# Layer 2's first product by Strassen's scheme in the last two passes, with split weights stored and fetched

## The chip, the core and the metric

The kernel runs on one core of a Trainium2 chip. A core has a matrix engine (PE; its weight loads are shown apart as PEld), three engines for elementwise work (DVE, ACT, POOL), and a queue for transfers (SP). Each runs its own instructions in the order in which the program lists them, and waits for the others by semaphores. The metric is the device time of one execution in microseconds (us).

## What is computed

Attention with a hash mask, then two feed-forward layers on 1536 tokens of width 512:

```python
x = attention(q, k, v, proj)                       # 1536 x 512
g = x @ w_gate; x = (g * sigmoid(g) * (x @ w_val)) @ w_out        # layer 1, d_ff 1536
h = x @ w_in                                       # layer 2, first product, 512 x 2048
g = max(h, 0) + alpha * min(h, 0)
out = g @ w_out2                                   # layer 2, second product, 2048 x 512
```

All inputs are float32.

## The kernel before

The tokens are cut into three chunks of W = 512. Attention runs interleaved with stage 1 (layer 1) of the first two chunks; then come stage 1 of chunk 2 and three passes of `stage2` (layer 2), for the chunks 1, 2 and 0. Chunk 0 is kept in device memory meanwhile (`spill`) and read back after the first pass. Only the last 270 us, stage 1 of chunk 2 and the three passes, are touched by most of the change.

Every product works on split numbers: a high part h (ACT copies to the matmul type, `split_h`, `w_h`) and a low part l, the rest (DVE or POOL subtracts, `split_l`, `w_l`). A product is three matmuls, h h, h l and l h (`mm3`, L699 to L701; `mm_out`, L704 to L706).

In `stage2`, F2 = 16 blocks f of 128 rows of h are made one after another. A block is 4 k-blocks x 3 matmuls of 512 columns into one PSUM bank (tags G, Y, G, po in turn). DVE forms the leaky g (`leak`, `leak_sum`), ACT and POOL split it (`gh`, `gl`), and D2 = 3 blocks later 12 matmuls add it to four output banks (tags S, S, S, T). At the end of a pass ACT and DVE copy these to `ob`, and SP stores them.

The weights come as a sequence `seq` of tiles (128 x 512) that `w_next` takes one by one. `w_ahead` runs in front of it by the numbers of `LEAD`: load, convert, high part, low part. For layer 2 the converted weights stay in SBUF (`fin.w`); each pass splits all 32 tiles anew, into `wb2` tiles with WB[2] = 6 buffers. Twelve of the 32 were converted early and are read from `whole` (L587); the rest are fetched raw and converted during stage 1 and the first pass (`w_late`, L596 to L601).

A scheduler sets the order of each engine's instructions from the program and the dependencies; a few are pinned. A tile's buffer is taken over once all readers of its last holder are done.

## Time and profile before

| | us |
|---|---|
| median of 3 runs (844.59 to 848.46) | 845.87 |
| the profiled execution | 843.88 |
| its span | 842.0 |

The page of the profile gives for each engine its busy time; further views give the same for a stretch, single instructions in order of time, waits, and the cost of groups of instructions by line. A matmul's busy time contains the wait for its pipeline, so matmuls overlap in the records; the distance between two starts is what one costs. The passes of layer 2 lie at 575.4 to 663.7, 663.7 to 750.7 and 750.7 to 837.7 us of the span.

### The profile page before, as it was taken

What the parts mean: (1) busy time and instruction counts of PE and PEld (TensorE: products, weight loads), DVE (VectorE), ACT (ScalarE), POOL (GpSimd) and SP (SyncE); (2) the same over time, 40 slices, a digit from 0 to 9 for tenths busy, and PEclk for the clock granted to TensorE, in tenths of its full rate; (3) what the DMA queues carried; (4) which work ended last, traced back from release to release, by engine and by line L of the source; (5) the groups of instructions that cost most, each with busy time, mean ns of one, the idle gap of its engine ahead of it and who ended that gap; (6) DMA issues with size and microseconds to landing.
All of it is one profiled execution on the core that took longest, in us unless ns stands there. A gap on an engine that the chain in (4) does not pass through costs nothing.

```text
span 842.0 us, 11156 instructions
## 1 busy us (share of the span) xinstructions
PE 813.0 (97%) x3988; PEld 681.7 (81%) x3988; DVE 536.6 (64%) x826; ACT 442.7 (53%) x738; POOL 347.5 (41%) x284
## 2 busy tenths in 40 slices
PE   5998899998999999999999999999999999999998
PEld 4777778887888888888888888887888888888886
DVE  5889998887898866656675342348986533334332
ACT  7889877877766645555544232224433333333331
POOL 5133337666755633222221352333543354445441
PEclk9999999999999999999999999999999999999999
DMA  9223346867656547554554787784300300010001
GB/s 246 69 69 98 128 120 203 253 220 241 219 202 234 174 152 260 199 179 149 175 188 141 249 286 235 262 282 170 138 1 0 151 1 0 1 51 1 0 1 51
DMA packets 57287, 122.03 MB, mean 145 GB/s; under 512 B 16912, under 2 KB 29200, under 8 KB 56720
## 3 DMA queue, kind: packets, MB, share of 16 engines
q1 hardware_dynamic: 56080, 118.51, 42.3%
q0 software_dynamic: 1008, 2.75, 1.6%
q8 instruction: 32, 0.52, 0.3%
q14 instruction: 23, 0.19, 0.1%
q10 hardware_dynamic: 144, 0.05, 0.0%
HBM read 94.03 MB, written 27.26 MB: 144 GB/s over the span
## 4 chain that ended last, share of the span: by engine, by line
PE 70%; DVE 9%; DMA 7%; ACT 7%; issue 4%; POOL 1%; SPq 0%; DVEq 0%; ACTq 0%; POOLq 0%
PE po L358 9%; PE gp L699 8%; PE gp L701 8%; PE gp L700 8%; PE op L705 5%; PE op L706 5%; PE op L704 5%; DMA raw<-in_wblk_dram 5%; PE hp L700 5%; PE hp L699 5%; PE hp L701 5%; PE S L304 2%; PE S L305 2%; ACT se L306 2%; DVE wt L599 1%
## 5 line engine op out<-in xcount | busy, mean ns | idle before, releaser
L694 POOL TENSOR_TENSOR gl<-ex,gh 128x512 fp32r<-128x512 f32 x81 | 110.2, 1360 | 191.8 <-ACT gh L691 174.5
L358 PE MATMUL po<-se,vv 128*128 128x256 f32 x576 | 139.2, 381 | 5.4 <-ACT se L347 2.8
L691 ACT ACTIVATE gh<-ex 128x512 fp32r<-128x512 f32 x84 | 53.0, 631 | 137.1 <-DVE ex L688 86.6
L358 PEld LDWEIGHTS po<-se,vv 128*128 128x128 f32 x576 | 106.2, 190 | 22.7 <-ACT se L347 4.6
L699 PE MATMUL gp<-xh,wb 128*128 128x512 f32 x288 | 120.1, 417 | 0.5 <-ACT xh L383 0.5
L701 PE MATMUL gp<-xh,wb 128*128 128x512 f32 x288 | 112.9, 392 | 0.0
L700 PE MATMUL gp<-xl,wb 128*128 128x512 f32 x288 | 112.7, 391 | 0.0
L636 ACT ACTIVATE wb<-w 128x512 fp32r<-128x512 f32 x96 | 59.7, 628 | 71.4 <-PE hp L701 57.6
L601 POOL TENSOR_TENSOR wt<-wt,wr 128x512 int32<-128x512 int32 x48 | 63.4, 1327 | 81.1 <-DVE wt L599 32.8
L685 DVE TENSOR_SCALAR ex<-hp,al 128x512 f32<-128x512 f32 x48 | 35.9, 748 | 93.2 <-PE hp L701 92.0
L306 ACT ACTIVATE se<-S 128x512 f32<-128x512 f32 x144 | 81.9, 593 | 23.7 <-PE S L305 22.7
L304 PE MATMUL S<-QA,kt 128*128 128x256 f32 x288 | 79.6, 303 | 6.8 <-ACT se L306 3.0
L341 DVE SCALAR_TENSOR_TENSOR se<-se,mb 128x1536 f32<-128x1536 f32 x48 | 83.5, 1740 | 3.4 <-PE mb L336 3.4
L347 ACT ACTIVATE se<-se 128x1536 f32<-128x1536 f32 x48 | 71.1, 1482 | 8.8 <-DVE se L341 8.6
L705 PE MATMUL op<-wb,gh 128*128 128x512 f32 x192 | 74.8, 390 | 0.9 <-DVE wb L643 0.9
L305 PE MATMUL S<-qb,kt 76*128 76x256 f32 x288 | 73.9, 286 | 1.0 <-ACT kt L218 0.6
L706 PE MATMUL op<-wb,gl 128*128 128x512 f32 x192 | 74.7, 389 | 0.0
L699 PE MATMUL hp<-xh,wb 128*128 128x512 f32 x192 | 74.7, 389 | 0.0
L700 PE MATMUL hp<-xl,wb 128*128 128x512 f32 x192 | 74.7, 389 | 0.0
L701 PE MATMUL hp<-xh,wb 128*128 128x512 f32 x192 | 74.7, 389 | 0.0
L704 PE MATMUL op<-wb,gh 128*128 128x512 f32 x192 | 74.7, 389 | 0.0
L643 DVE TENSOR_TENSOR wb<-w,wb 128x512 fp32r<-128x512 f32 x65 | 56.1, 866 | 17.4 <-ACT wb L636 17.4
(99 smaller groups left out, 1666.7 us busy)
## 6 DMA issues: line engine op xcount, KB each, us to landing
wb<-w SPq DMA_DIRECT2D x72, 512.0 KB, 4.1
raw<-in_wblk_dram SPq DMA_DIRECT2D x68, 512.0 KB, 4.6
w<-wb SPq DMA_DIRECT2D x36, 512.0 KB, 3.0
qr<-in_q_dram SPq DMA_DIRECT2D x24, 256.0 KB, 2.9
nat<-in_k_dram SPq DMA_DIRECT2D x8, 384.0 KB, 3.4
vv<-in_v_dram SPq DMA_DIRECT2D x16, 192.0 KB, 5.6
whole<-wt SPq DMA_DIRECT2D x12, 256.0 KB, 2.2
w<-whole SPq DMA_DIRECT2D x12, 256.0 KB, 4.3
```

The source lines that it names most:

```text
L304: nc.tensor.matmul(pt[:, i, :], lhsT=ka[:, sl], rhs=qa, start=True, stop=False)
L305: nc.tensor.matmul(pt[:, i, :], lhsT=kb[:, sl], rhs=qb, start=False, stop=True)
L306: nc.scalar.activation(out=u.se[:, 2 * j:2 * j + 2, :], in_=pt, func=AF.Copy)
L341: ins = nc.vector.scalar_tensor_tensor(out=u.se, in0=u.se, scalar=FLOOR, in1=u.mx[:, None, :].to_broadcast([P, NC, GQ]), op0=ALU.max, op1= ...
L358: nc.tensor.matmul(it.po[:, u.x, :], lhsT=VV[it.b, it.p][:, kb, u.x * D:u.x * D + P], rhs=u.se[:, kb, :], start=kb == 0, stop=kb == NC - 1)
L694: eng.tensor_tensor(out=l, in0=ex, in1=f32(h), op=ALU.subtract)
L699: nc.tensor.matmul(pt, lhsT=h, rhs=ah, start=first, stop=False)
L700: nc.tensor.matmul(pt, lhsT=h, rhs=al_, start=False, stop=False)
L701: nc.tensor.matmul(pt, lhsT=l, rhs=ah, start=False, stop=last)
L704: nc.tensor.matmul(pt, lhsT=gh, rhs=h, start=first, stop=False)
L705: nc.tensor.matmul(pt, lhsT=gh, rhs=l, start=False, stop=False)
L706: nc.tensor.matmul(pt, lhsT=gl, rhs=h, start=False, stop=last)
```

## The change

The first pass stays as it is, but stores each split tile in device memory (`split`). The second and third pass (`wino`, for the chunks 2 and 0) take two blocks f as a 2 x 2 matrix of weights (two blocks f by two halves of k) and the chunk as a 2 x 2 matrix (two halves of k by two halves of 256 tokens), and form the result from seven products instead of eight, in Winograd's form. Each product is 2 k-blocks x 3 matmuls, now of 256 columns: 42 matmuls a pair of blocks where there were 24 of 512.

The scheme needs sums of weights: two further tiles a pair, made by `w_sums` on DVE from `fin.w`, split by `w_h` and `w_l`, during the second pass, and stored; the third pass fetches them. All other tiles of both passes are fetched (`w_load`). It needs four sums of x (`sums`, split too): those of chunk 2 are made in the first pass from `acc`, those of chunk 0 at the end of the second pass, from an `acc` that is spilled and read back. It needs additions after the products: per pair five on DVE (two of 512 columns, three of 256) after one copy by ACT. The leaky function becomes two Relus on ACT and one step on DVE. POOL splits the low part of g in the middle of the second pass, DVE elsewhere; low parts of layer 2's weights are all DVE's.

The core of the diff:

```diff
...
-LEAD = ((2, 2, 3, 5), (4, 5, 5, 7))
+LEAD = ((2, 2, 3, 5), (4, 5, 5, 7), (4, 4, 5, 6))
...
+    def order2w():
+        o = []
+        for j in range(F2 // 2):
+            o += [F2I + 2 * j, F2S + 2 * j]
+            o += [F2I + F2 + 2 * j - 3] if j > 1 else []
+            o += [F2S + 2 * j + 1]
+            o += [F2I + F2 + 2 * j - 2] if j else []
+            o += [F2I + 2 * j + 1]
+        return o + list(range(F2I + 2 * F2 - 3, F2I + 2 * F2))
+    F2S = F2I + 2 * F2
     o2 = order2()
+    o2w = order2w()
     early = o2[:sum(EARLY)]
     late = [w for w in o2 if w not in early]
-    seq = order1() * NP2 + o2 * NP2
+    seq = order1() * NP2 + o2 + o2w * (NP2 - 1)
     NWT = len(seq)
-    NW1 = NWT - len(o2) * NP2
-    fresh = [w not in seq[:i] for i, w in enumerate(seq)]
-    new = [n or w >= F2I for n, w in zip(fresh, seq)]
+    NW1 = len(order1()) * NP2
+    NW2 = NW1 + len(o2)
+    new = [w not in seq[:i] for i, w in enumerate(seq)]
+    fresh = [n and w < F2S for n, w in zip(new, seq)]
+    split = [dram.tile([P, 2, 512], F32, name=f"s{i}") for i in range(3 * F2)]
     raw, wt, ready = {}, {}, {}
     ws = Bag()
...
             pass
         elif fresh[i] and w in early:
             pin(nc.sync.dma_start(out=fin.w[:, w - F2I, :], in_=whole[w - F2I]))
         elif fresh[i]:
             raw[i] = raw_load(w)
-        elif w < F2I:
-            nc.sync.dma_start(out=f32(w_tile(i)), in_=scratch[w])
+        elif not new[i]:
+            nc.sync.dma_start(out=f32(w_tile(i)), in_=scratch[w] if w < F2I else split[w - F2I])
     def round64(t, a):
...
+        return fin.w[:, w - F2I, n * HW:(n + 1) * HW]
+    def w_sums(i):
+        j, kind = divmod(seq[i] - F2S, 2)
+        f = F2I + 2 * j
+        t = wt[i] = wp.tile([P, 512], F32, tag="wt", name="wt", bufs=WB[0])
+        ops = ((t[:, 0:HW], quarter(f + 1, 0), quarter(f + 1, 1), ALU.add),
+               (t[:, HW:], t[:, 0:HW], quarter(f, 0), ALU.subtract)) if kind == 0 else (
+               (t[:, 0:HW], quarter(f, 0), quarter(f + 1, 0), ALU.subtract),
+               (t[:, HW:], quarter(f, 1), ws.s2, ALU.subtract))
+        if kind == 0:
+            ws.s2 = t[:, HW:]
+        for o, x, y, op in ops:
+            nc.vector.tensor_tensor(out=o, in0=x, in1=y, op=op)
     def w_conv(i):
         w = seq[i]
-        if w >= F2I:
+        if not new[i]:
+            pass
+        elif w >= F2S:
+            w_sums(i)
+        elif w >= F2I:
             wt[i] = fin.w[:, w - F2I, :]
         elif fresh[i]:
             wt[i] = wp.tile([P, 512], F32, tag="wt", name="wt", bufs=WB[0])
...
             n, m = PL
-            eng = nc.gpsimd if i % n < m and not ws.late else nc.vector
+            eng = nc.gpsimd if i < NW1 and i % n < m else nc.vector
             eng.tensor_tensor(out=ready[i][:, 1, :], in0=wt.pop(i), in1=f32(ready[i])[:, 0, :], op=ALU.subtract)
     def w_put(i):
-        if fresh[i] and seq[i] < F2I:
-            nc.sync.dma_start(out=scratch[seq[i]], in_=f32(ready[i]))
+        if new[i]:
+            w = seq[i]
+            nc.sync.dma_start(out=scratch[w] if w < F2I else split[w - F2I], in_=f32(ready[i]))
     def upto(name, n, fn):
         n = min(n, NWT)
...
     def w_ahead(n):
-        lead = LEAD[n >= NW1]
+        lead = LEAD[(n >= NW1) + (n >= NW2)]
         for name, k, fn in (("load", 2, w_load), ("conv", 1, w_conv), ("h", 0, w_h)):
             upto(name, n + lead[0] + k, fn)
         upto("l", n + lead[0], w_l)
...
-    def stage2(c, conv):
+    def sums(acc, ts):
+        def x(k, t):
+            return acc[:, 2 * k:2 * k + 2, t * HW:(t + 1) * HW]
+        f = {}
+        for name, a, b in (("1", lambda: x(0, 1), lambda: x(0, 0)), ("2", lambda: x(1, 1), lambda: f["1"]),
+                           ("4", lambda: x(1, 0), lambda: f["2"]), ("3", lambda: x(1, 1), lambda: x(0, 1))):
+            t = f[name] = wp.tile([P, 2, HW], F32, tag="wr", name="tf", bufs=2)
+            tc.keep_in_program_order(nc.vector.tensor_tensor(out=t, in0=a(), in1=b(), op=ALU.subtract))
+            hl = wp.tile([P, 2, 512], F32R, tag="wb", name="ts", bufs=WB[1])
+            h, l = ts[name] = [hl[:, i, :].rearrange("p (k e) -> p k e", e=HW) for i in range(2)]
+            tc.keep_in_program_order(nc.scalar.activation(out=h, in_=t, func=AF.Copy))
+            (nc.gpsimd if name == "4" else nc.vector).tensor_tensor(out=l, in0=t, in1=f32(h), op=ALU.subtract)
+            yield
+    def out_block(fo, gs, ops):
...
+        a, b_ = gs.pop(fo)
+        if fo == 0:
+            ops.extend(at.ps.tile([P, 512], F32, tag=t, name="op", bufs=at.nb[t]) for t in "SSST")
+        for i in range(W // P):
+            sl = slice(i * P, (i + 1) * P)
+            mm_out(ops[i], a[:, sl], b_[:, sl], h, l, fo == 0, fo == F2 - 1)
+    def out_all(c, ops):
+        for i in range(W // P):
+            out_rows(c * W + i * P, ops[i], i, fin.pool.tile([P, W], F32, tag="ob", name="ob", bufs=4))
...
+    def wino(c, ts, side):
         xh, xl = chunk(c)
-        t0 = c * W
+        def x(k, t):
+            return [v[:, 2 * k:2 * k + 2, t * HW:(t + 1) * HW] for v in (xh, xl)]
+        def product(pt, i, w, n, b):
+            for k in range(2):
+                kk = 2 * n + k
+                mm3(pt[:, i, :], (w[0][:, kk, :], w[1][:, kk, :]), b[0][:, k, :], b[1][:, k, :], k == 0, k == 1)
+        def bank(tag):
+            return at.ps.tile([P, 2, HW], F32, tag=tag, name="hp2", bufs=at.nb[tag])
+        def leaky(f, v):
+            ex = tmp()
+            g = gs[f] = g_tiles()
+            nc.scalar.activation(out=ex, in_=v, func=AF.Relu)
+            nc.scalar.activation(out=v, in_=v, func=AF.Relu, scale=-1.0)
+            nc.vector.scalar_tensor_tensor(out=ex, in0=v, scalar=aln[:, f:f + 1], in1=ex, op0=ALU.mult, op1=ALU.add)
+            split_h(g[0], ex)
+            split_l(g[0], g[1], ex, nc.gpsimd if side and 2 <= f < F2 - 2 else nc.vector)
+        add = ALU.add
+        ops, gs = [], {}
+        for j in range(F2 // 2):
+            pq = fin.pool.tile([P, 2, HW], F32, tag="ob", name="pq", bufs=4)
+            r = wp.tile([P, 4, HW], F32, tag="raw64", name="rs", bufs=RAWB)
+            wa, wb = w_next(), w_next()
+            pt = bank("G")
+            product(pt, 0, wa, 0, x(0, 0))
+            product(pt, 1, wb, 0, ts["1"])
+            nc.scalar.activation(out=pq, in_=pt, func=AF.Copy)
+            pt = bank("Y")
+            product(pt, 0, wb, 1, ts["2"])
+            product(pt, 1, wa, 1, x(1, 0))
+            nc.vector.tensor_tensor(out=r[:, 0:2, :], in0=pt, in1=pq[:, 0:1, :].to_broadcast([P, 2, HW]), op=add)
+            nc.vector.tensor_tensor(out=r[:, 3, :], in0=r[:, 0, :], in1=pq[:, 1, :], op=add)
+            if j == F2 // 2 - 1:
+                for _ in "12":
+                    next(side or iter(()), 0)
+            if j > 1:
+                out_block(2 * j - 3, gs, ops)
+            wb = w_next()
+            pt = bank("G")
+            product(pt, 0, wb, 0, ts["3"])
+            product(pt, 1, wb, 1, x(1, 1))
+            nc.vector.tensor_tensor(out=r[:, 0:3:2, :], in0=pt, in1=r[:, 0::3, :], op=add)
+            x2 = tmp()
+            nc.vector.tensor_tensor(out=x2[:, HW:], in0=r[:, 0, :], in1=pq[:, 1, :], op=add)
+            leaky(2 * j, r[:, 1:3, :].rearrange("p a b -> p (a b)"))
+            if j:
+                out_block(2 * j - 2, gs, ops)
+            wb = w_next()
+            pt = bank("po")
+            product(pt, 0, wb, 1, ts["4"])
+            nc.vector.tensor_tensor(out=x2[:, 0:HW], in0=pt[:, 0, :], in1=r[:, 0, :], op=add)
+            leaky(2 * j + 1, x2)
+        for _ in side or ():
+            pass
+        for f in range(F2 - 3, F2):
+            out_block(f, gs, ops)
+        out_all(c, ops)
...
+                out_block(f - D2, gs, ops)
+            if f % 3 == 2:
+                next(side, 0)
+        out_all(c, ops)
...
-    spill = dram.tile([2, P, KD * W], F32, name="spill")
+    spill = dram.tile([3, P, KD * W], F32, name="spill")
...
-            for i, t in enumerate(chunk(0)):
-                nc.sync.dma_start(out=spill[i], in_=f32(t).rearrange("p k w -> p (k w)"))
+            for i, t in enumerate([f32(t) for t in chunk(0)] + [at.acc]):
+                nc.sync.dma_start(out=spill[i], in_=t.rearrange("p k w -> p (k w)"))
...
         pass
-    for n, c in enumerate((1, 2, 0)):
-        if n == 1:
-            CH.pop(0)
-            for i, t in enumerate(chunk(0)):
-                nc.sync.dma_start(out=f32(t).rearrange("p k w -> p (k w)"), in_=spill[i])
-        ws.late = n == 0
-        stage2(c, late_steps)
+    ts = [{}, {}]
+    aln = fin.pool.tile([P, F2], F32, name="aln")
+    nc.scalar.activation(out=aln, in_=al, func=AF.Copy, scale=-1.0)
+    ws.late = True
+    stage2(1, late_steps, sums(at.acc, ts[0]))
+    ws.late = False
+    CH.pop(0)
+    for i, t in enumerate(chunk(0)):
+        nc.sync.dma_start(out=f32(t).rearrange("p k w -> p (k w)"), in_=spill[i])
+    acc = at.lt.tile([P, KD, W], F32, tag="acc", name="acc", bufs=1)
+    nc.sync.dma_start(out=acc.rearrange("p k w -> p (k w)"), in_=spill[2])
+    wino(2, ts[0], sums(acc, ts[1]))
+    wino(0, ts[1], None)
 # ---- launch: one core; inputs and outputs as the reference has them ----
...
```

What it does to the order of instructions, at three places. In the order `hp_...` is a PSUM bank of the first product, `op` an output bank, `wb_...` a weight tile with its number, `wt` and `w` unsplit weights, `ts` a split sum of x, `rs` and `pq` the additions' tiles, `ex` the leaky tile. Lines of after are those of the changed file.

PE, at the start of the second pass. Before, the pass's first bank ends and the second begins, each with 12 matmuls of 512 columns:

```order
L701 MATMUL hp_6164<-xh,wb_6089 128x512
L699 MATMUL hp_6164<-xh,wb_6089 128x512
L700 MATMUL hp_6164<-xl,wb_6089 128x512
L701 MATMUL hp_6164<-xh,wb_6089 128x512
L699 MATMUL hp_6187<-xh,wb_6104 128x512
L700 MATMUL hp_6187<-xl,wb_6104 128x512
```

After, the second pair's third bank (`hp_6405`, 12 matmuls on the sums tile `wb_6346`), one matmul of its seventh product, and then the pass's first output block:

```order
L739 MATMUL hp_6405<-xl,wb_6346 128x256
L740 MATMUL hp_6405<-xh,wb_6346 128x256
L738 MATMUL hp_6405<-xh,wb_6346 128x256
L739 MATMUL hp_6405<-xl,wb_6346 128x256
L740 MATMUL hp_6405<-xh,wb_6346 128x256
L738 MATMUL hp_6453<-ts,wb_6344 128x256
L743 MATMUL op<-wb_6311,gh 128x512
L744 MATMUL op<-wb_6311,gh 128x512
L743 MATMUL op<-wb_6311,gh 128x512
L744 MATMUL op<-wb_6311,gh 128x512
L743 MATMUL op<-wb_6311,gh 128x512
L745 MATMUL op<-wb_6311,gl 128x512 x2
```

A bank of the first product is now made of two products of six matmuls, and the first output block follows the second pair's third bank.

ACT and DVE at that place. Before, on DVE, behind the copies of the first pass's outputs:

```order
L713 COPY ob<-op 128x512 x2
L643 TENSOR_TENSOR wb_6189<-w_4721,wb_6189 128x512
L685 TENSOR_SCALAR ex_6180<-hp_6164,al 128x512
L688 SCALAR_TENSOR_TENSOR ex_6180<-hp_6164,ex_6180 128x512
L685 TENSOR_SCALAR ex_6203<-hp_6187,al 128x512
```

After, on DVE, from the end of the first pair:

```order
L893 TENSOR_TENSOR ex_6334<-rs,pq 128x256
L900 TENSOR_TENSOR ex_6334<-hp_6349,rs 128x256
L880 TENSOR_TENSOR rs<-hp_6384,pq 128x512
L681 TENSOR_TENSOR wb_6346<-wt,wb_6346 128x512
L863 SCALAR_TENSOR_TENSOR ex_6336<-rs,aln,ex_6336 128x512
L863 SCALAR_TENSOR_TENSOR ex_6357<-ex_6334,aln,ex_6357 128x512
L881 TENSOR_TENSOR rs<-rs,pq 128x256
L733 TENSOR_TENSOR gl<-ex_6336,gh 128x512
```

After, on ACT, from the copy of the first pair's first bank:

```order
L876 ACTIVATE pq<-hp_6282 128x512
L674 ACTIVATE wb_6316<-wt 128x512
L876 ACTIVATE pq<-hp_6370 128x512
L861 ACTIVATE ex_6336<-rs 128x512
L674 ACTIVATE wb_6346<-wt 128x512
L862 ACTIVATE rs<-rs 128x512
L861 ACTIVATE ex_6357<-ex_6334 128x512
L862 ACTIVATE ex_6334<-ex_6334 128x512
L730 ACTIVATE gh<-ex_6336 128x512
```

The split of `wb_6346` stands behind work on the second pair's banks `hp_6370` (its first, on ACT) and `hp_6384` (its second, on DVE).

DVE between stage 1 and the first pass. Before:

```order
L740 TENSOR_TENSOR xl<-acc,xh 128x512
L643 TENSOR_TENSOR wb_5475<-w_4721,wb_5475 128x512
L736 TENSOR_TENSOR acc<-gp,acc 128x512
L740 TENSOR_TENSOR xl<-acc,xh 128x512
L736 TENSOR_TENSOR acc<-gp,acc 128x512
L740 TENSOR_TENSOR xl<-acc,xh 128x512
```

After:

```order
L681 TENSOR_TENSOR wb_5526<-w_4770,wb_5526 128x512
L775 TENSOR_TENSOR acc<-gp,acc 128x512
L635 TENSOR_TENSOR wt<-wt,w_4770 128x256
L635 TENSOR_TENSOR wt<-w_4770 128x256
L635 TENSOR_TENSOR wt<-w_4770,wt 128x256
L779 TENSOR_TENSOR xl<-acc,xh 128x512
L775 TENSOR_TENSOR acc<-gp,acc 128x512
L635 TENSOR_TENSOR wt<-w_4770 128x256
L635 TENSOR_TENSOR wt<-wt,w_4770 128x256
L779 TENSOR_TENSOR xl<-acc,xh 128x512
```

Five sums of weights now stand between the steps that make the x of the first pass.

## Rows read from the trace of the kernel before

**Rows 1.** Page, part 1: busy us, share of the span, instructions.

```profile
PE 813.0 (97%) x3988; PEld 681.7 (81%) x3988; DVE 536.6 (64%) x826; ACT 442.7 (53%) x738; POOL 347.5 (41%) x284
```

**Rows 2.** Busy us, the three passes: PE, PEld, DVE, ACT, POOL; clock, DMA share, GB/s.

```profile
575.40:663.70 88.30, 87.35 (x386) 72.04 (x385) 70.05 (x86) 35.43 (x61) 35.63 (x26) 1.00 0.25 91
663.70:750.70 87.00, 87.00 (x385) 72.06 (x384) 33.36 (x50) 31.37 (x51) 40.64 (x32) 1.00 0.04 13
750.70:837.70 87.00, 87.00 (x385) 71.91 (x383) 32.01 (x48) 28.25 (x46) 36.88 (x29) 1.00 0.03 12
```

**Rows 3.** Waits of PE from 540 us on: total us, times, longest.

```profile
PE op L705 <- DVE wb L643: 0.9, 1, 0.9
```

**Rows 4.** PE in order of time, second pass: start us, us, instruction.

```profile
690.86 0.39 PE L704 MATMUL op<-wb,gh 128*128 128x512 f32 x1
691.09 0.39 PE L705 MATMUL op<-wb,gh 128*128 128x512 f32 x1
```

**Rows 5.** PE in order of time, attention beside stage 1.

```profile
420.59 0.39 PE L701 MATMUL gp<-xh,wb 128*128 128x512 f32 x1
420.82 0.28 PE L304 MATMUL S<-QA,kt 128*128 128x256 f32 x1
...
421.66 0.28 PE L305 MATMUL S<-qb,kt 76*128 76x256 f32 x1
421.78 0.40 PE L699 MATMUL gp<-gh,wb 128*128 128x512 f32 x1
422.02 0.40 PE L700 MATMUL gp<-gl,wb 128*128 128x512 f32 x1
```

**Rows 6.** PE's weight loads in order of time, same stretch.

```profile
420.94 0.19 PEld L304 LDWEIGHTS S<-QA,kt 128*128 128x128 f32 x1
```

**Rows 7.** Groups by line, last two passes: busy us, mean ns, idle before.

```profile
L694 POOL TENSOR_TENSOR gl<-ex,gh 128x512 fp32r<-128x512 f32 x32 | 41.3, 1290 | 78.0 <-ACT gh L691 78.0
L636 ACT ACTIVATE wb<-w 128x512 fp32r<-128x512 f32 x59 | 37.3, 632 | 60.4 <-PE hp L701 53.8 <-PE op L706 4.5
L688 DVE SCALAR_TENSOR_TENSOR ex<-hp,ex 128x512 f32<-128x512 f32 x32 | 21.9, 684 | 0.2
L643 DVE TENSOR_TENSOR wb<-w,wb 128x512 fp32r<-128x512 f32 x30 | 21.1, 704 | 4.2 <-ACT wb L636 4.1
```

**Rows 8.** Groups by line and shape, whole span: 256 columns on DVE, PSUM copies on ACT.

```profile
L380 DVE TENSOR_TENSOR xf<-po,den 64x256 f32<-64x256 f32 x48 | 20.1, 419 | 1.4
L328 DVE TENSOR_TENSOR m<-m 128x256 f32<-128x256 f32 x30 | 15.6, 519 | 0.0
...
L715 ACT ACTIVATE ob<-op 128x512 f32<-128x512 f32 x6 | 3.6, 598 | 8.9 <-PE op L706 8.9
```

**Rows 9.** POOL and DVE in order of time, first pass.

```profile
613.29 1.42 POOL L694 TENSOR_TENSOR gl<-ex,gh 128x512 fp32r<-128x512 f32 x1 [3.21 <-issue]
...
613.71 1.55 DVE L643 TENSOR_TENSOR wb<-w,wb 128x512 fp32r<-128x512 f32 x1 [0.16 <-ACT wb L636]
```

**Rows 10.** DMA issues (KB, median us to landing), and GB/s in 40 slices of 300:330.

```profile
wb<-w SPq DMA_DIRECT2D x72, 512.0 KB, 4.1
...
spill<-xl SPq DMA_DIRECT2D x1, 1024.0 KB, 8.1
...
GB/s 77 0 0 0 0 0 0 0 71 404 224 142 371 186 91 258 0 82 262 382 377 426 360 437 404 350 229 213 289 415 415 366 426 137 27 16 0 109 322 284
```

**Rows 11.** PE and DVE in order of time, stage 1 to first pass; idle before in brackets.

```profile
575.16 0.39 PE L701 MATMUL gp<-gh,wb 128*128 128x512 f32 x1
...
577.65 0.39 PE L700 MATMUL hp<-xl,wb 128*128 128x512 f32 x1
...
574.90 0.69 DVE L740 TENSOR_TENSOR xl<-acc,xh 128x512 fp32r<-128x512 f32 x1 [0.70 <-ACT xh L738]
575.58 0.69 DVE L736 TENSOR_TENSOR acc<-gp,acc 128x512 f32<-128x512 f32 x1
576.97 0.69 DVE L740 TENSOR_TENSOR xl<-acc,xh 128x512 fp32r<-128x512 f32 x1 [0.70 <-ACT xh L738]
```

More of the change, by code (lines that the diff above doesn't have):

```diff
@@ L82, in lsh_attention_moe_kernel @@
     W = 512
+    HW = W // 2
     NP2 = B * S // W
@@ L583, in w_load @@
         w = seq[i]
-        if w in late:
+        if w in late and new[i]:
             pass
@@ L745, in stage1 @@
         xh, xl = chunk(c)
-        acc = at.lt.tile([P, KD, W], F32, tag="acc", name="acc", bufs=1)
+        acc = at.acc = at.lt.tile([P, KD, W], F32, tag="acc", name="acc", bufs=1)
         gs = {}
@@ new lines, in out_block @@
+    def out_block(fo, gs, ops):
+        h, l = flat(w_next())
+        a, b_ = gs.pop(fo)
[7 more added lines that the diff above has]
+            out_rows(c * W + i * P, ops[i], i, fin.pool.tile([P, W], F32, tag="ob", name="ob", bufs=4))
@@ L777, in stage2 @@
+    def stage2(c, conv, side=iter(())):
+        xh, xl = chunk(c)
         ops, gs = [], {}
@@ L792, in stage2 @@
             if f >= D2:
-                fo = f - D2
-                h, l = flat(w_next())
-                a, b_ = gs.pop(fo)
-                if fo == 0:
-                    ops = [at.ps.tile([P, 512], F32, tag=t, name="op", bufs=at.nb[t]) for t in "SSST"]
-                for i in range(W // P):
-                    sl = slice(i * P, (i + 1) * P)
-                    mm_out(ops[i], a[:, sl], b_[:, sl], h, l, fo == 0, fo == F2 - 1)
-        for i in range(W // P):
-            out_rows(t0 + i * P, ops[i], i, fin.pool.tile([P, W], F32, tag="ob", name="ob", bufs=4))
+                out_block(f - D2, gs, ops)
+            if f % 3 == 2:
+                next(side, 0)
+        out_all(c, ops)
     fin = Bag()
```

1 line of the change is left out of this document (added).

## The prediction

> **What bounds the kernel now.** I read the page's busy times first, then the busy times of the three passes of layer 2, PE's waits there, single instructions in order of time, and last the cost per instruction and the transfers. PE is busy 97% of the span [rows 1], and each of the last three passes of layer 2 takes 87.0 us (the first 88.3) with PE busy throughout, at full granted clock, while DVE, ACT and POOL are at 40% in the last two passes and the DMA share is 0.04 [rows 2]. From 540 us to the end PE waits once, 0.9 us [rows 3]. So nothing but PE's own work sets the length of the passes, and what the change takes off PE there is worth its full time, as long as the other engines, which get new work, stay hidden.
>
> The busy column of PE is no price: a matmul is shown as 389 ns, but matmuls overlap. What counts is the distance between starts. 512 columns: 690.86 to 691.09 [rows 4]; over a pass 87.0 us / 384 matmuls = 226.6 ns. 256 columns of the same type: the S products of attention, eight starts from 420.82 to the next instruction's 421.78, 120 ns each [rows 5]. That is more than half of 226.6 by 6.7 ns.
>
> **Part by part: the matmuls.** Before, two blocks f cost 2 x 4 x 3 = 24 matmuls of 512 columns, 24 x 226.6 = 5.44 us. After, seven products of two k-blocks and three terms, 42 matmuls of 256 columns. The 120 ns come from a stretch in which 512 columns also start 0.23 to 0.24 apart [rows 5], a little over the quiet rows, so I bound the price by 118 and 120 and take 119: 42 x 119 = 5.00 us. The gain is 0.44 us a pair, times 8 pairs and 2 passes: **-7.1 us** (-6.4 at 120, -7.8 at 118). The second product keeps its 24 matmuls a pair, so a pair with it lasts 10.44 us.
>
> Each of the 42 also loads 128x128 weights, 190 ns in the record [rows 6]. The S rows do that at every 120 ns, on full 128-row weights every second time, so I take no price for it.
>
> The Trainium skill (TensorE: Matmul & The Clock Gate, Part 2, "Back-to-back issue gap") gives an isolated distance of N/2.4 + 2.5 ns, that is 109 and 216 ns. By it the gain would be (24 x 216 - 42 x 109) x 16 = 9.7 us; the rows here read 120 and 227, and no wait lies in them, so this figure stays out of the sum.
>
> **The start of the second pass.** Here the new work is not hidden. The sums of weights for this pass are made and split while it runs, six wb2 buffers at a time. The fourth tile of sums (called wb_6346 in the order) goes into the buffer of the first pair's last tile, free after 42 matmuls, at 5.0 us of the pass; and its split stands, on ACT, behind the eviction of the second pair's first bank and a Relu, on DVE behind the next bank's first sum (order rows of ACT and DVE in the section on the change). With t from the pass's first product: that bank is full after 54 matmuls, 6.4; an eviction starts 0.2 behind the stream (the matmul starting at 575.16 and the DVE sum at 575.58, less 0.23 [rows 11]); 0.60 for the copy [rows 8], 0.6 each for Relu and high part [rows 7]: high part at 8.4. DVE waits for the Y bank, full after 66 matmuls, 7.9, its sum 0.69, then the low part 0.69: 9.4. PE wants this tile at 7.9 and its low part two matmuls later, 8.1. **+1.3 us**, once. Below: 0, if ACT reaches it between (the buffer is free at 5.2 and 0.6 + 0.7 would fit); above: 3, if the first output block, which stands behind it and needs the same two engines' split of g, is late too; it is ordered high parts first, so I count it as covered.
>
> **Steady pairs.** The chain from a bank to the split g (DVE sum 0.69, two Relus 1.2, DVE 0.68, ACT 0.63, POOL 1.29 [rows 7], with handovers some 6 us) has 10.5 us for an even f (the output block stands a pair later) and 13 for an odd one: hidden. A weight buffer is free 2.9 us into its pair and wanted again at 10.44, 7.5 us, against 4.1 from issue to landing of 512 KB [rows 10]. What it costs if that cover goes is a rival below. Third pass: no sums to make, all six tiles of a pair fetched; the loads queue on SP behind the second pass's four output stores, but the first behind them is wanted 5.8 us into the pass: 0, up to 1.
>
> **Between stage 1 and the first pass.** The DVE order gets five sums of 256 columns between the last two acc and xl steps. DVE idles 0.70 us twice there, and xl of the last k-block, started 576.97 and about 0.6 long, is wanted by the matmul at 577.65 [rows 11]: no slack. A 256-column sum takes 0.42 to 0.52 [rows 8]; three in the first gap overrun it by 0.6 us, of which the acc step, which waits for PE anyway, passes on some 0.5: **+0.5 us** (0 to 1.3).
>
> **The rest.** In the first pass DVE, 70 us busy of 88 [rows 2], gets seven more steps for the sums of x; SP gets 32 stores of 512 KB in front of the raw weights; attention gets one more spill of 1 MB, and such a one took 8.1 us [rows 10]. Splitting in the last two passes goes away, but ACT, DVE and POOL were covered there, so that is worth 0. I put +0.3 for all of it (-0.5 to +1.5).
>
> Sum: -7.1 + 1.3 + 0.5 + 0.3 = -5.0 us. The profiled execution took 843.9 us (span 842.0 and 1.9 around it): 838.9. The median of the runs, 845.9, lies 2.0 above that execution, and the median is what will be compared: **840.9 us**, 0.6% faster. What a measurement of this kernel can tell from no change is about 0.5%, 4.2 us.
>
> **Rivals.**
> Nothing stalls: the scheduler's order leaves the start covered and the quiet price of 118 holds, -7.8 us: 838.1. For it: the rows show PE waiting 0.9 us in 300. Against: the order of ACT and DVE at the start of the pass.
>
> DVE becomes the bound in the second pass. A pair there needs three sums out of PSUM (0.69 + 0.69 + 0.42), two of 256 in SBUF, four of weights (six times 0.42 to 0.52), two leaky steps and two low parts (4 x 0.69): 7.1 to 7.7 us. A DVE step with two SBUF inputs waits while POOL computes: 0.69 became 1.55 beside a POOL step that ran until 614.71 [rows 9], and two POOL steps of 1.29 stand in each pair. With both, 9.7 to 10.3 of 10.44. If the order costs 0.3 to 0.6 us a pair over eight pairs and the start loses 3, the gain is down to 0 to -3: 843 to 846, no change. It decides as soon as DVE is late by more than the 4 us that the chain of g leaves.
>
> Loads too late, the slower case. The last two passes moved 13 GB/s [rows 2]; now six tiles of 512 KB per 10.44 us, 301 GB/s, loads and in the second pass stores, in one SP queue in which a store that waits for a low part holds the loads behind it. Slices of a stretch with two 1 MB spills show up to 437 GB/s [rows 10], so it should fit, but under that load a 1 MB transfer took 8.1. From a landing of 7.5 us on each pair waits; at 8.5 it is 16 x 1 us: 857.
>
> Weight loads do not overlap. If each 256-column matmul waited for its 190 ns of loading [rows 6], 42 x 309 = 13.0 us instead of 5.44 a pair, 16 times +7.5 us: 966. The S rows at 120 ns speak against it. It is the rule of the Trainium skill (TensorE: Matmul & The Clock Gate, Part 3, "The mechanism") that a load overlaps running matmuls only where the row groups differ; the trace does not agree.
>
> **How the numbers follow.** Forecast 0.45 (own range 839.0 to 842.5), no stall 0.15, DVE-bound 0.28, loads late or a stall that I do not see 0.11, weight loads 0.01. Faster by over 0.5% is below 841.7: no stall and most of the forecast, 0.15 + 0.38. Within: the rest of the forecast and most of the DVE case, 0.07 + 0.27. Slower: 0.13. The range leaves out the fastest tenth and what is above the DVE case: 836.5 to 847.0.
>
> **What would show it.** The 256-column products should start 118 to 120 ns apart, and the last two passes last about 83.5 us each (8 pairs of 10.44) instead of 87.0, the second with its wait on top. Right: one PE wait of 1 to 2 us on a weight tile's split in the second pair of the second pass, nothing after. DVE-bound: PE waits on DVE's split in most pairs. Loads: PE waits on a DMA of a weight tile. Wrong at the root: a distance well above 120 ns.

## The result and the profile after

The changed kernel takes 851.84 us (median of 6 runs, 850.05 to 852.76) where the kernel before takes 845.85 in the same job: 1.0067 of it, interval 1.0048 to 1.0085. Forecast were 840.9, range 836.5 to 847.0: wrong in sign. The profiled spans are 849.9 and 842.0.

Busy times on the page:

```profile
PE 813.8 (96%) x4276; PEld 695.7 (82%) x4276; DVE 586.9 (69%) x923; ACT 462.7 (54%) x779; POOL 283.6 (33%) x235
```

The three passes (limits at the first and last matmul of each, rounded to 0.1 us; columns as in [rows 2]), then 3.4 us inside the first and the second:

```profile
579.20:671.10 91.90, 88.97 (x385) 73.22 (x385) 77.81 (x102) 35.77 (x62) 36.36 (x26) 0.98 0.75 278
671.10:761.00 89.90, 86.48 (x529) 78.05 (x528) 63.08 (x105) 44.52 (x77) 17.68 (x13) 0.98 0.89 316
761.00:845.70 84.70, 84.48 (x529) 76.20 (x527) 43.57 (x74) 34.51 (x59) 0.00 (x0) 1.00 0.81 283
593.50:596.90 3.40, 3.40 (x8) 2.72 (x9) 3.40 (x6) 2.24 (x4) 1.51 (x1) 0.50 0.92 301
678.80:682.20 3.40, 3.40 (x16) 3.40 (x17) 3.40 (x8) 0.98 (x3) 0.00 (x0) 0.51 1.03 422
```

Against [rows 2] the first pass has grown from 88.3 to 91.9 us, although its matmuls are unchanged, the second from 87.0 to 89.9, and only the third gained, 87.0 to 84.6 (84.7 by the rounded limits of the row). The DMA share in the last two passes went from 0.04 and 0.03 to 0.89 and 0.81. The clock column says 0.98 in two passes; the last two rows show why: 3.4 us at half the clock (1.2 instead of 2.4 GHz), where 8 matmuls of 512 or 16 of 256 columns start, about half the usual number. Each costs about 1.7 us.

What PE waits for from 540 us on (as [rows 3], where one wait of 0.9 us stood):

```profile
PE op L744 <- DVE wb L681: 2.9, 1, 2.9
PE hp L738 <- ACT pq L876: 2.4, 1, 2.4
PE hp L740 <- DVE wb L681: 1.0, 1, 1.0
PE hp L738 <- DMA wb<-s: 0.2, 1, 0.2
```

The first two waits on PE in order of time:

```profile
593.44 0.77 PE L744 MATMUL op<-wb,gh 128*128 128x512 f32 x1 [2.93 <-DVE wb L681]
594.00 0.63 PE L745 MATMUL op<-wb,gl 128*128 128x512 f32 x1
594.43 0.63 PE L743 MATMUL op<-wb,gh 128*128 128x512 f32 x1
...
678.71 0.49 PE L738 MATMUL hp<-xh,wb 128*128 128x256 f32 x1 [2.42 <-ACT pq L876]
679.01 0.42 PE L739 MATMUL hp<-xl,wb 128*128 128x256 f32 x1
679.22 0.42 PE L740 MATMUL hp<-xh,wb 128*128 128x256 f32 x1
```

ACT at the second:

```profile
670.62 0.60 ACT L754 ACTIVATE ob<-op 128x512 f32<-128x512 f32 x1 [0.76 <-PE op L745]
678.06 0.60 ACT L876 ACTIVATE pq<-hp 128x512 f32<-128x512 f32 x1 [6.84 <-DMA out_dram<-ob]
```

The transfers between 660 and 685 us (GB/s in 40 slices; KB, median us to landing):

```profile
GB/s 98 413 328 282 374 184 0 334 393 151 315 419 393 433 361 426 472 380 210 262 210 380 413 420 419 393 387 410 413 413 433 416 426 413 426 361 66 0 0 131
...
wb<-s SPq DMA_DIRECT2D x7, 512.0 KB, 6.7
s<-wb SPq DMA_DIRECT2D x5, 512.0 KB, 7.4
xh<-spill SPq DMA_DIRECT2D x1, 1024.0 KB, 5.6
xl<-spill SPq DMA_DIRECT2D x1, 1024.0 KB, 9.4
out_dram<-ob SPq DMA_DIRECT2D x4, 256.0 KB, 8.0
```

The copy `pq` lies in the buffers of the output tiles `ob` (tag "ob"), so ACT stands 6.8 us until an output store of the first pass has landed. Before, these took 2.1 us; now they took 8.0, between reloads, stores and fetches. PE waits for the bank that `pq` empties, and half clock follows (the distances of 0.21 us behind 679.01).

### The profile page after: what moved, and what is told of

Same layout as the page of the kernel before. It is cut to its first block, busy times and chain, and to the rows that moved or that the text cites. A ratio compares the mean times of both kernels' runs of the same rounds, so it can differ in the third digit from the quotient of the medians.

```text
span 849.9 us, 12128 instructions
## 1 busy us (share of the span) xinstructions
PE 813.8 (96%) x4276; PEld 695.7 (82%) x4276; DVE 586.9 (69%) x923; ACT 462.7 (54%) x779; POOL 283.6 (33%) x235
## 4 chain that ended last, share of the span: by engine, by line
PE 70%; DVE 10%; ACT 7%; DMA 6%; issue 4%; POOL 1%; SPq 0%; DVEq 0%; ACTq 0%; POOLq 0%
PE po L359 9%; PE gp L738 8%; PE gp L740 8%; PE gp L739 8%; PE op L744 5%; PE op L745 5%; PE op L743 5%; PE hp L740 4%; PE hp L738 4%; PE hp L739 4%; DMA raw<-in_wblk_dram 3%; PE S L305 2%; PE S L306 2%; ACT se L307 2%; ACT se L348 1%
## 5 line engine op out<-in xcount | busy, mean ns | idle before, releaser
L733 POOL TENSOR_TENSOR gl<-ex,gh 128x512 fp32r<-128x512 f32 x61 | 84.7, 1389 | 175.4 <-ACT gh L730 115.9
L305 PE MATMUL S<-QA,kt 128*128 128x256 f32 x288 | 81.9, 311 | 8.5 <-ACT se L307 6.4
L342 DVE SCALAR_TENSOR_TENSOR se<-se,mb 128x1536 f32<-128x1536 f32 x48 | 83.5, 1740 | 3.5 <-PE mb L337 3.5
L744 PE MATMUL op<-wb,gh 128*128 128x512 f32 x192 | 75.9, 396 | 2.9 <-DVE wb L681 2.9
L743 PE MATMUL op<-wb,gh 128*128 128x512 f32 x192 | 75.6, 394 | 0.0
L305 PEld LDWEIGHTS S<-QA,kt 128*128 128x128 f32 x288 | 56.4, 196 | 15.7 <-ACT se L307 8.9
L740 PEld LDWEIGHTS gp<-xh,wb 128*128 128x128 f32 x288 | 54.1, 188 | 11.9
L738 PEld LDWEIGHTS gp<-xh,wb 128*128 128x128 f32 x288 | 54.3, 189 | 10.1 <-ACT xh L384 1.1
L739 PEld LDWEIGHTS gp<-xl,wb 128*128 128x128 f32 x288 | 54.4, 189 | 9.1
L612 ACT ACTIVATE wr<-raw 128x512 int32<-128x512 uint32 x68 | 45.4, 668 | 29.1 <-DMA raw<-in_wblk_dram 20.8
L738 PE MATMUL gp<-gh,wb 128*128 128x512 f32 x144 | 60.6, 421 | 0.0
```

The source lines that it names most:

```text
L305: nc.tensor.matmul(pt[:, i, :], lhsT=ka[:, sl], rhs=qa, start=True, stop=False)
L342: ins = nc.vector.scalar_tensor_tensor(out=u.se, in0=u.se, scalar=FLOOR, in1=u.mx[:, None, :].to_broadcast([P, NC, GQ]), op0=ALU.max, op1= ...
L733: eng.tensor_tensor(out=l, in0=ex, in1=f32(h), op=ALU.subtract)
L738: nc.tensor.matmul(pt, lhsT=h, rhs=ah, start=first, stop=False)
L739: nc.tensor.matmul(pt, lhsT=h, rhs=al_, start=False, stop=False)
L740: nc.tensor.matmul(pt, lhsT=l, rhs=ah, start=False, stop=last)
```

## The experiments

All times in us; passes from first to last matmul of the one profiled execution; waits of PE of 0.5 us and more, summed by kind. The ratio is to the kernel before in the same job. The outputs of e6 are not the reference's; it only shows what the time hangs on.

| run | median | ratio, 95% | three passes | PE waits for |
|---|---|---|---|---|
| changed | 851.84 | 1.0067 [1.0048, 1.0085] | 91.9, 89.9, 84.6 | split 2.9; pq 2.4; split 1.0 |
| e1 pq alone | 848.43 | 1.0031 [1.0014, 1.0049] | 90.4, 88.4, 86.5 | split 2.5; fetches 2.6 and 2.1 |
| e2 sums in order | 851.34 | 1.0063 [1.0039, 1.0087] | 90.5, 95.2, 86.0 | split 1.9; pq 3.4; fetches 4.0; split 1.2 |
| e3 e1 and e2 | 849.81 | 1.0040 [1.0022, 1.0057] | 89.6, 88.8, 85.3 | split 0.9; fetches 2.7; gl 0.6; split 0.5 |
| e4 stores first | 852.46 | 1.0077 [1.0054, 1.0099] | 90.3, 92.7, 85.6 | split 2.4; high part 5.6; fetch 1.0 |
| e5 e1, reload spread | 849.10 | 1.0017 [0.9998, 1.0036] | 89.2, 90.0, 88.3 | split 1.3; fetches 1.7 and 2.4; splits 1.8 |
| e6 e1, most traffic out | 841.07 | 0.9928 [0.9908, 0.9949] | 89.9, 84.4, 84.1 | split 2.4 |
| e7 store and fetch alone | 846.61 | 0.9998 [0.9983, 1.0013] | 89.7, 87.0, 87.0 | split 2.3 |
| e8 e1, 4 fetches, POOL | 846.43 | 1.0004 [0.9988, 1.0020] | 92.9, 86.5, 84.7 | high part 2.7; split 1.0; gh 0.7 |
| e9 e1, ACT's queue, POOL | 849.56 | 1.0041 [1.0025, 1.0057] | 93.1, 86.7, 85.4 | fetches 2.6; high part 2.0; split 0.6 |
| e10 e8 and e9 | 845.85 | 0.9993 [0.9976, 1.0010] | 92.3, 86.6, 84.1 | high part 2.1; split 1.0; gh 0.8 |
| e11 e10, sums in order | 849.39 | 1.0035 [1.0016, 1.0053] | 92.9, 90.2, 84.1 | gh 3.9; splits 1.2 and 0.5; gl 0.6 |
| e12 e7, POOL | 844.05 | 0.9980 [0.9964, 0.9996] | 88.6, 87.0, 87.0 | split 0.6 |
| e13 e1, 4 fetches | 844.78 | 0.9987 [0.9974, 1.0001] | 89.9, 86.7, 84.3 | splits 1.4; gh 0.9; gl 0.6 |
| e14 e13, ACT's queue | 844.16 | 0.9975 [0.9962, 0.9988] | 91.2, 87.0, 84.1 | split 2.3; gh 1.1 |

**The two waits, each alone and together (e1 to e3), and the order of the stores (e4).**

```diff
# e1 (and e3)
-            pq = fin.pool.tile([P, 2, HW], F32, tag="ob", name="pq", bufs=4)
+            pq = wp.tile([P, 2, HW], F32, tag="wr", name="pq", bufs=2)
# e2 (and e3)
-            nc.vector.tensor_tensor(out=o, in0=x, in1=y, op=op)
+            tc.keep_in_program_order(nc.vector.tensor_tensor(out=o, in0=x, in1=y, op=op))
# e4: keep_in_program_order around the output stores and the reloads of xh and xl
```

> The low part of the second pass's first weight tile (pq) gets buffers of its own; in the changed kernel it shares four with the output tiles and so waits until the first pass's outputs are stored. Theory: the 2.4 us wait at the start of the second pass goes, and with it the 3.4 us of half clock behind it (worth 1.8): second pass 85.5 to 86.5 us after 89.9, median about 848 after 851.8. Rival 1: something else is late at the same place (the split of the first tile, 1 us), so that only 1 to 1.5 us come back: 850.5. Rival 2: the wait was on something other than the stores, pq comes as late as before: 851.8.

> The sums of weight tiles (w_sums, on DVE) keep their place in the program, so that none of them stands between stage 1 and the first pass. Theory: DVE reaches the first output weight tile's split in time, TensorE's wait of 2.9 us in the first pass falls to about 1 us (as in the kernel before) and the half clock behind it goes: first pass about 88.3 us after 91.9, median about 848. Rival: DVE was late for another reason (the weight load that lands 1.1 us later, 5.7 after 4.6), the wait stays at 2 us or more: 851 to 852. If the sums at the end of the pass make the spill of them late, the second pass is longer by what the first one gains.

> Both edits, pq in buffers of its own and the sums in program order. Theory: the two stalls are independent, each with its own half clock: first pass 88.3, second 85.5 to 86.5, third 84.6, median about 844.2 after 851.8, 0.2% under the kernel before at 845.9. Rival: the gains do not add, since the time is bound by something both share (the DMA queues, DVE): 848 or more.

> Buffers stay shared; the two 1 MB reloads of the chunk's activations are issued on SP behind the four output stores of the first pass and not ahead of them. Theory: the stores land about 2 us after issue as in the kernel before, not 5 to 8 us, the low part of the first weight tile is made in time, second pass about 86, median about 848 to 849. Rival: the stores wait behind the other traffic of the weights (stores and fetches) and not behind these two reloads: landing 5 us or more, second pass still 88 to 90, median 851 to 852. A third: the later reloads themselves come late, third pass longer.

The expectations of e1 and e4 call `pq` the low part of a weight tile. It is the copy of a pair's first bank, as the diff has it, and that is what e1 edits.

e1 comes out at 848.4, as expected (about 848), but not in the way expected: the wait on `pq` is gone, a wait of the same size stands in its place, and one has come at the third pass:

```profile
674.35 0.55 PE L738 MATMUL hp<-xh,wb 128*128 128x256 f32 x1 [2.61 <-DMA wb<-s]
```

SP of e1 at the third pass, which begins at 754.9 (SP's rows show issues):

```profile
754.31 2.68 SPq L755 DMA_DIRECT2D out_dram<-ob x4
757.07 16.38 SPq L607 DMA_DIRECT2D wb<-s x12
```

Behind the output stores stand the fetches, of which PE wants one 5.6 us into the pass. The two waits differ: the fetch at the second pass was issued at 663.46, 3.1 us before the pass, and landed 10.8 us later; the one at the third was issued only at 757.07 and landed in 5.8. So rival 1 was right that something else is late at the same place, but it is a fetch and not a split. e2 does not bring the gain: the wait in the first pass is 1.9, and the second pass is longer, 95.2. That the moved sums do this is not shown: e3 has them in the same order and a second pass of 88.8, and the profiled execution of e2 is the slowest of its six (853.71). e3 does not add the gains up, as its rival said. e4 brings no gain from the order of the stores: they land in 4.5 us instead of 8.0, but `pq` still stands 4.3 us for one, and ACT now makes the high part of the second pair's first sums tile behind the first pair's Relus and `gh`, which come late; PE waits 5.6 us for it.

**Is it the transfers? (e5, e6, e7)**

```diff
# e5: e1, and the reload of chunk 0 in eight pieces of 256 KB, two in each of the pairs 1 to 4
+            if 1 <= j <= 4:
+                next(back, 0)
+                next(back, 0)
...
# e6: e1, and from the ninth tile on one resident tile; most stores and the reload left out
-        elif not new[i]:
+        elif not new[i] and i < NW2 + 8:
...
+        t = ready.pop(i) if i in ready else ws.res
# e7: the plain passes on stored and fetched tiles
-    seq = order1() * NP2 + o2 + o2w * (NP2 - 1)
+    seq = order1() * NP2 + o2 * NP2
...
+    stage2(2, iter(()))
+    stage2(0, iter(()))
```

> pq in buffers of its own (as in e1), and the two 1 MB reloads of chunk 0 cut into eight pieces of 256 KB that are issued in the pairs 1 to 4 of the second pass, not at the end of the first. Theory: at the start of the second pass the transfers are the bound (about 8 MB in 25 us at 320 to 420 GB/s in e1 and e4), and whatever is made to wait for less there, the next thing waits for a transfer that stands behind the 2 MB. With them gone the 2.6 us wait on a fetch in e1 and the half clock behind it go: second pass 84 to 85 us after 88.4, median about 845 after e1's 848.4. Rival: the stores and fetches of weights alone fill the queues (301 GB/s steady), the wait stays at 2 us or more, second pass 87 to 89, median 848. Third case: the pieces delay the fetches behind them in the pairs 1 to 4, and PE waits there.

> The traffic taken away: from the ninth weight tile of the second pass on, the tiles that the changed kernel fetches are one resident tile (so the outputs of these passes are not the reference's), the first pass stores only the few tiles that are still fetched, the sums are made and split but not stored, and chunk 0 is not reloaded (the third pass works on chunk 2 again); pq in buffers of its own. Arithmetic on all engines is the changed kernel's. Theory: all waits on transfers at the pass changes go, second and third pass 83.6 to 84.5 us each, first pass 88 to 89, median about 842. Rival: the remaining loss is DVE's and ACT's work and order (sums, splits, additions), the second pass stays above 87 us without any traffic, median 847 or more.

> The other part alone: the first pass stores its 32 split tiles, the second and third fetch them, and both work as before the change (24 matmuls of 512 columns a pair of blocks, no sums of weights or of x). Theory: the steady fetches cost nothing (512 KB per 2.7 us, 193 GB/s), second and third pass 87.0 to 88 each with a wait at the start of the second where the reload stands in front; the stores in the first pass cost what DVE's lateness costs, so 846 to 849. Rival: storing and fetching itself costs most of what the changed kernel loses (waits on fetches in many blocks): 851 or more.

The second and third pass of e6:

```profile
668.00:752.40 84.40, 84.40 (x529) 76.31 (x528) 62.00 (x105) 45.02 (x77) 18.32 (x13) 1.00 0.11 40
752.40:836.50 84.10, 84.10 (x529) 76.11 (x527) 44.09 (x76) 34.40 (x59) 0.00 (x0) 1.00 0.04 15
```

And of e7:

```profile
665.20:752.20 87.00, 87.00 (x385) 72.05 (x384) 24.47 (x34) 11.28 (x19) 20.64 (x16) 1.00 0.64 221
752.20:839.30 87.10, 87.10 (x385) 71.88 (x383) 24.47 (x34) 11.37 (x19) 20.64 (x16) 1.00 0.55 177
```

In e6 PE is busy for the whole of both passes, with the changed kernel's work on DVE (62 us), ACT and POOL: with most transfers gone nothing stands still in the second and third pass. In e7 the fetches, four tiles a pair and not six, cost nothing there. So the products alone gain 5.5 us, four fetches a pair alone are free in these passes, and products with six fetches gain nothing. e6 takes away the rate, the places in SP's queue and the turns of the weight buffers at once, so it does not tell which of them it is; the two fetches of e1 above show one late by its landing and one by its issue. e5 asks about the reload: with it out of the way PE still waits for fetches, 1.7 at the second pass and 2.4 at the third, and for splits. The view of waits puts the 1.7 down to a `gl` step of DVE; but PE's next load waits for the semaphore of the fetch issued at 668.90, which landed at 676.85, and PE goes on at 676.98. The reload is not the one cause; its rival holds, with a second pass of 90.0.

**Fewer fetches, and the first pass (e8 to e14).**

```diff
# e8, e10, e11, e13, e14: tiles of the second product split anew in each pass, not stored
+    new = [n or F2I + F2 <= w < F2S for n, w in zip(new, seq)]
...
# e8 to e12: the low part that POOL made in stage 1 is POOL's again
-            eng = nc.gpsimd if i < NW1 and i % n < m else nc.vector
+            eng = nc.gpsimd if i < NW2 and i % n < m and not ws.late else nc.vector
# e9, e10, e11, e14
-        nc.sync.dma_start(out=out[r0:r0 + P, :], in_=ob)
+        nc.scalar.dma_start(out=out[r0:r0 + P, :], in_=ob)
# e11: also e2's edit
```

> As e1, but the 16 tiles of the second product are split anew from SBUF in every pass, as before the change (ACT 0.63 and DVE 0.68 us a tile); only the tiles of the first product are stored and fetched, four a pair where there were six (200 GB/s steady instead of 301; e7 moved 193 and showed no wait on a transfer). The one low part of layer 2 that POOL made in stage 1 before the change is POOL's again. Theory (the loss is in the transfers): second and third pass 84 to 85.5 us each after 88.4 and 86.5 in e1; the wait of PE in the first pass falls from 2.5 towards 1; median about 843.5. Rival: DVE, with 11 us more in each pass, becomes late, PE waits on splits (wb <- DVE) several times in the second pass: 847 or more.

> As e1, but the output stores are issued on ACT's queue, so that no fetch stands behind them on SP (and POOL makes the one low part as in e8). Theory of the order: in e1 the fetch that PE waits for at the start of the third pass is issued 2.2 us after the pass begins, behind four output stores that wait for the copies of the outputs; issued at the pass's start it lands in time: third pass 84.5 after 86.5, the wait there gone; the wait at the start of the second pass stays, since the 2 MB reload stands in front of it: about 846.5. Rival: the transfers' rate is what binds and not the place in the queue: both waits stay, 848. Or ACT loses what SP gains by issuing: later splits and copies, 848 to 850.

> Both, e8 and e9. Theory: the two act on the same waits, so that little is added to e8: 842 to 844, second and third pass 84 to 85 us, no wait above 1 us but the one in the first pass. Rival: DVE's late splits bind, as in e8's rival: 847 or more.

> e10 with the sums of weights kept in program order, so that between stage 1 and the first pass DVE and POOL stand as before the change: one low part on POOL, no sum in between. In the runs so far PE's wait in the first pass follows the place of DVE's first rounding step after the start of the pass, one for one (2.2 us after it: wait 0.9, in the kernel before and e3; 2.6: 1.3, e5; 3.6 to 3.8: 2.3 to 2.5, e1, e4, e6, e7; 4.2: 2.9, the changed kernel). Theory: that step comes at 2.2, the wait is 0.9, no half clock follows, first pass 88.5 to 89 after e10's 92.3; second and third as in e10, 86.6 and 84.1; median 842 to 843 after 845.9. Rival: DVE waits for raw weights that land later beside the new stores, the wait stays at 2 us: 845.

> e7 (store and fetch, no Strassen, no sums) with the one low part given back to POOL; no other line. Theory: in e7 DVE stands for 1.9 us at the first split of layer 2 in stage 1, waiting for ACT's copy of a weight that has just landed, and the steps for x come that much later; before the change POOL stood there and DVE went on. With POOL's step back the wait of PE in the first pass falls from 2.3 to about 1 us, first pass 88.3 after 89.65, median 845 to 846. Rival: the stores of the first pass make the raw weights land late and PE waits 2 us all the same.

> e1 with one more edit: the 16 tiles of the second product are split anew in every pass, four tiles a pair are fetched and not six. Theory (transfers are the loss in the last two passes, DVE's place the loss in the first): first pass as in e1, 89 to 90.5, second and third as in e8, 86.5 and 84.7, median 844 to 845, under the kernel before by 0.2 to 0.3%, and 4 under e1's 848.4. Rival: the gain of e8 in the last two passes came from its other order, and with e1's first pass the waits on fetches or splits return: 847 or more.

> e13 with the output stores on ACT's queue. Theory: third pass 84.1 as in e10 and not 84.7, the rest as e13: 843.5 to 844.5. Rival: no difference to e13 that can be told, or ACT's later steps cost as much: 845 or more.

With four fetches a pair the last two passes take 86.5 to 87.0 and 84.1 to 84.7 us in e8, e10, e13 and e14, although DVE has more to do (e13):

```profile
666.20:752.90 86.70, 85.53 (x529) 76.02 (x528) 74.60 (x121) 51.70 (x93) 17.83 (x13) 1.00 0.61 213
752.90:837.20 84.30, 84.30 (x529) 76.10 (x527) 53.84 (x91) 43.58 (x75) 0.20 (x1) 1.00 0.53 183
```

No wait on a fetch of 0.5 us is left. The rival of a late DVE falls in the third pass; in the second about 2 us remain, 1.2 of them waits on splits of g at its end. e8, e9 and e10 missed their medians, with first passes of 92.3 to 93.1; e13 and e14, without the line for POOL, hit theirs, though e14 with a first pass of 91.2 and not the 89.9 of e13. e14 is a quarter of a per cent faster than the kernel before, the fastest version with the scheme whose outputs are whole, but its interval overlaps that of e13, so ACT's queue is not shown to matter there. Nor is that gain shown to come from the scheme: e12, which has no Strassen products, comes out at 0.9980.

The third pass is 86.5 in e1 and 85.4 in e9, where no fetch stands behind output stores: the fetch that PE waits for is issued 0.2 us into the pass and not 2.2, and the wait is 0.5 and not 2.1. With four fetches the third pass is 84.7 and 84.3 with SP's queue (e8, e13) and 84.1 with ACT's (e10, e14). The Trainium skill (DMA: Bandwidth & Descriptors, "Issuing engines are not separate DMA queues") says that issuing from several engines saves only the time of issuing. The rows of e1 show another thing that it saves here: the fetches issued at 757.07 stood in SP's queue behind stores that waited for ACT's and DVE's copies of the outputs.

For the first pass, ACT and DVE of e7 at the end of stage 1:

```profile
570.84 1.95 ACT L674 ACTIVATE wb<-w 128x512 fp32r<-128x512 f32 x3 [1.94 <-DMA w<-whole]
...
571.51 0.69 DVE L681 TENSOR_TENSOR wb<-w,wb 128x512 fp32r<-128x512 f32 x1 [1.88 <-ACT wb L674]
572.12 0.69 DVE L775 TENSOR_TENSOR acc<-gp,acc 128x512 f32<-128x512 f32 x1
```

ACT, DVE and POOL of e12 there:

```profile
571.54 1.94 ACT L674 ACTIVATE wb<-w 128x512 fp32r<-128x512 f32 x3 [1.34 <-DMA w<-whole]
...
571.57 0.69 DVE L775 TENSOR_TENSOR acc<-gp,acc 128x512 f32<-128x512 f32 x1 [0.65 <-PE gp L740]
...
572.25 1.30 POOL L681 TENSOR_TENSOR wb<-w,wb 128x512 fp32r<-128x512 f32 x1 [7.60 <-ACT wb L674]
```

In e7 DVE stands 1.9 us for a weight that has not landed, and the `acc` step behind it comes late; in e12 POOL stands there and DVE goes on. PE's waits fall from 2.3 to 1.0 us (0.6 on DVE, 0.4 on ACT), the pass from 89.7 to 88.6. No sums are made in either kernel. That the line did this is not shown. The weight landed 4.7 us before the pass in e7 and 5.3 in e12. With e12's landing, DVE's first rounding step in e7 (the pass's first step on raw weights) would come 0.6 us sooner, 3.0 us after the start of the pass by this estimate, and that is where it comes in e12. The rest is a later such step that took 0.69 us and not 1.67, with no POOL step beside it. The intervals of the two medians overlap.

Seven kernels show what this place hangs on: the changed one, e1, e4, e5, e6, e13 and e14 have the same order of instructions on DVE, ACT and POOL from the start of the kernel to 10 us into the first pass, sums included, and the same transfers in front of it. DVE of the changed kernel and of e5, first split and first rounding step (the passes start at 579.25 and 576.58):

```profile
575.30 0.69 DVE L681 TENSOR_TENSOR wb<-w,wb 128x512 fp32r<-128x512 f32 x1 [1.94 <-ACT wb L674]
583.45 0.42 DVE L613 TENSOR_SCALAR w<-raw 128x512 int32<-128x512 int32 x1
...
571.00 0.69 DVE L681 TENSOR_TENSOR wb<-w,wb 128x512 fp32r<-128x512 f32 x1 [0.30 <-ACT wb L674]
579.15 0.42 DVE L613 TENSOR_SCALAR w<-raw 128x512 int32<-128x512 int32 x1
```

In the seven DVE stands 0.15 (e13) to 1.94 us (changed) at that split. The rounding step comes 2.26 us plus that after the start of the pass, and PE's first wait is the step's place less about 1.25 us. The fetch of that weight is issued 10.3 us before the pass in all of them and before the change alike; it landed 5.7 us later in the changed kernel, 3.9 in e13, 4.2 before the change. e13 and e14 have 0.15 and 1.28. So this wait differs between executions of one order, and the first passes of single profiles differ by it.

With the scheme, the line that gives the split back to POOL moved sums and raw steps (e8 to e10), and PE waited more. In e11, with the sums kept in place, DVE's first rounding step comes 2.2 us after the start as before the change, and PE's first wait is down to 0.5 us; but gh is late at the ends of the first two passes (3.9 us in all), and the median of 849.4 misses the 842 to 843 expected.

## Why the prediction was wrong, point by point

The step that failed is what must land before an instruction can start. The sum put the transfers at nothing ("so it should fit"), let the eviction start "0.2 behind the stream", and looked between stage 1 and the first pass only at the sums. What the runs show in its place is PE waiting behind a store that took 8.0 us to land (`pq`, 2.4 us of PE) and a fetch that took 10.8 (e1, 2.6 us): with most traffic gone (e6) the last two passes take 168.5 us, with all of it and `pq` freed (e1) 174.9, against 174.0 before.

**The matmuls, -7.1:** the right mechanism, a quarter too large. In e6, where nothing waits, the passes take 84.4 and 84.1 us, not 83.5: the 256-column products start 119.7 ns apart (119 taken), and the second product's 512-column matmuls 229 instead of 226.6. Gain 2.6 + 2.9 = 5.5 us. (The prediction's own factors give 7.0, and 7.7 at 118 ns, each 0.1 less than it writes.) That loads of weights do not overlap (966 us) is excluded.

**The start of the second pass, +1.3:** the wait named there came, on the low part of `wb_6346`, 1.0 us. But in front of it stood the one that I had not seen, 2.4 us and half clock behind it: 5.5 us in all over the 84.4 of e6. What failed here is the eviction "0.2 behind the stream": I priced the copy `pq` by its bank and its engine, and did not ask whose buffer it writes. The diff has it, tag "ob", and the stores that hold that buffer are in the sentence on the third pass ("the loads queue on SP behind the second pass's four output stores"); I counted them there only.

**Steady pairs, hidden:** right. After the second pair of the second pass PE waits 0.2 us once, at the start of the third pass, and no more; landing took 4.9 us (median), where 7.5 were free.

**Third pass, 0 to 1:** 0.5 over e6 in the changed kernel, right; 2.4 in e1. The fetch goes out 1.4 us into the pass and lands in 4.7 us in the changed kernel, 2.2 and 5.8 in e1; why is not shown.

**Between stage 1 and the first pass, +0.5:** the wrong matmul, and too small. The `xl` that I followed belongs to chunk 2, which the second pass reads and not the first (the section on the change has that wrong too); PE did not stop there. But DVE came late, by 2.0 us (4.2 after the start of the pass, where it was 2.2), and 10 us later PE waited 2.9 us instead of 0.9 for the first output tile's split; with half clock the pass is 3.6 longer. The five sums that I priced are worth under 0.1 us of it: in the seven kernels with this order the step would come at 2.26 if DVE did not stand for the weight. The 1.94 that it stood are the rest. Before the change POOL stood there ("low parts of layer 2's weights are all DVE's"); I priced that move in the last two passes alone, at 0. Whether the move costs anything, or only the late landing does, stays open: the first rounding step of e7 and e12 comes out alike once their landings are counted, and e7's median is that of the kernel before (0.9998), although its first pass is 1.4 us longer in the profile.

**The rest, +0.3:** the profile shows the passes starting 3.9 us later. The twelve other runs that spill `acc` too, with nearly the same first 570 us, start them at 575.6 to 578.2, the kernels without that spill at 575.4 to 576.8. So most of the 3.9 is not shown to come from the change; whether the spill costs up to one us stays open.

Sum by the passes: -2.4 in the third, +2.9 in the second, +3.6 in the first, +4.1 together; with the 3.9 in front of them that is the 7.9 between the two profiled spans. The medians differ by 6.0: the profiled execution of the kernel before lies 2.0 under its median, so a difference of 1 or 2 us against its passes need not be the change's.

**Rivals.** "DVE becomes the bound" forecast 843 to 846 and is refuted by e6, where DVE does the same work and PE does not wait. "Loads too late" comes nearest: its size (857) and its place (every pair) are wrong, its resource is right. I compared a steady 301 GB/s with a peak and let it fit; but at the turn of a pass the reload, four output stores, stores of sums and fetches meet, and there the slices from 673 to 682 us read 361 to 433 GB/s. The Trainium skill (Perfetto Trace Analysis, "Roofline") puts the aggregate of a core's 16 DMA engines at about 435 GB/s; these slices lie under it, and one before them, 0.6 us long, reads 472. What this takes away is landing time: 512 KB landed in 4.1 us before, in 4.9 now (median), in 10.8 for the fetch in e1, and a 256 KB output store in 8.0 instead of 2.1.

## What to carry to other kernels

Price a transfer rate where transfers meet, not as a mean: four fetched tiles a pair (a pass at 177 to 221 GB/s) cost nothing in the last two passes here, six (285 to 319) cost the whole gain at their turns (e7 and e1). For each new tile ask whose buffer it takes and what must land before that is free, and for each step moved from one engine to another, what stands behind it when its input is late. A stall removed (e1, e3, e5) moves to the next late thing while the shared resource stays full; taking work from the resource (e13) left no wait on a transfer of 0.5 us. And compare more than one profile: the same order of instructions gave first waits of 1.2 to 2.9 us.
